# Retention and gated feed-forward on one core: columns 512 to 1023 as one block by seven quarter products, with a fourth token pair

## The chip, the cores and the metric

The kernel runs on one core of one Trainium2 chip. The metric is the device time of one execution in microseconds. Where a difference between two kernels is meant, the two are run in turn on the same chip and the ratio of their times is given.

## The reference

Inputs are q, k and v of shape (8, 8, 576, 64), that is batch, heads, tokens and head size, and three weights. All are float32; the output is (4608, 512) in float32.

```
scores = (q @ k^T) / sqrt(64)
Dmat   = gamma_h ** (i - j) where i >= j, else 0;  gamma_h = 1 - 2 ** (-5 - h)
attn   = (scores * Dmat) @ v                       # no softmax
x      = attn, heads side by side                  # (4608, 512)
out    = (sigmoid(x @ w_gate) * (x @ w_val)) @ w_out   # 512 -> 1536 -> 512
```

## The kernel before

**Columns and blocks.** x is kept transposed, 512 rows by token columns, in bfloat16. The 4608 columns are not in the order of the output rows: `rows_of` and `rows` say which output rows a column stands for. The feed-forward part goes through the columns in blocks: the first 512 columns are written out by hand, then `BLOCKS` (L366) lists two blocks of 256 columns (512 and 768) and seven of 512 (from 1024 on). TensorE's order is the order of the program: the schedule is manual, and each engine works its own list in order, waiting on semaphores.

**Retention.** Because the decay is a power, it is put into q and k by tables (`qtab`, `ktab`), and a running state per batch carries what earlier tokens give to later ones. Tokens are handled in two ways.

- A *pair* is 256 tokens of one batch, loaded with two neighbouring tokens in one partition. `PAIRS` (L102) names three: both halves of batch 0's first 512 tokens, and the first 256 tokens of batch 1. Pairs give columns 0 to 767. For a pair, `cast_pair` scales and casts (GpSimd for k and v, VectorE for q), `pair_t` turns k and q on TensorE (ScalarE copies the result out), `pair_qk` makes scores (VectorE masks them, tiles `ptp`), `third_intra` the values inside the pair, `pair_st` the state, `third_inter` the part that comes from the state, and `pair_out` and `third_out` the copies to x.
- A *step* is a chunk of 128 tokens (two pieces of 64). `STEPS` (L105) lists them; the first two are the chunks (1, 2) and (1, 3), which give columns 768 to 1023. `casts_to` loads ahead on the SP queue, scales k and q on GpSimd or VectorE, turns them (`cross`: a DMA transpose; `turn_step`, for the steps in `TURNED`, on TensorE), and casts v. `slot_of_two` does two steps at a time on TensorE: values of the two earlier ones (`intra`, `inter`), scores of the two new ones (`scores`), and what they add to the state (`products`). `after_two` adds states on VectorE and copies to x on ScalarE. Between the first and second half of `inter` a tiny operation on VectorE or ScalarE, the *glance*, reads the tile.

**Feed-forward.** A block of 256 columns is done by `h_units` (L879: per two rows of 128 of the hidden size, 8 matmuls of 256 columns for the gate, 8 for the value) and `op_units` (L1262: the output product, 512 columns a matmul). A block of 512 columns is done by `quarter_units` (L977): the product of a unit (4 x 128 hidden rows by 512 columns) is made of seven products of a quarter each, numbered 1 to 7 in the order strings. `g16` is product 6 of gate unit 1; `w03` is product 3 of value unit 0; `v9` is hidden row block 9 of the values as a plain product (`value`, L1063). Such a block needs sums of the weights (`w_sums`, tiles `wgt` and `wvt`) and four sums of x (`x_sums`, L960, tiles `xsum`): products 1, 2 and 3 read x itself, 5, 6, 7 and 4 read sums 1, 3, 2 and 4 of it in the order in which they are made. Results leave through ScalarE copies and VectorE additions (lines L999, L1044, L1052, L1055, L1040). From column 1024 on the output product of a block is also made of seven products (`quarters`, L1105), from sums of the hidden tile (`gsum`) and of the output weight (`wt_sb`).

**Order around the change.** After the first 512 columns' hidden part (`h_both`, L1325) comes their output product (`op_first`, L1484), cut into pieces between which pair 2's work stands (L1490 to L1533). Then the main loop (L1554) takes the blocks in turn. `SUMS_AT` (L1535) says at which piece of which block a weight sum, a `casts_to` or a `turn_step` is put, and `PAIRS_AT` (L1548) where the step pairs of the first four slots stand.

```
PAIRS = [(0, 0), (0, 1), (1, 0)]
STEPS = [(1, 2), (1, 3)]
BLOCKS = [(512, 256), (768, 256)] + [(t, 512) for t in range(1024, NT, 512)]
FIRST = ("g01 g05 g11 w05 g06 g15 g03 w01 g02 g16 g12 g07 w06 g13 g21 g17 w03 w11 w07 g14 g04 w02 w04 "
         "w16 w12 g26:0-1v w15:0-2v:0-3p w17 g25 g22 w13 g27:0-4v g23 w14:1-1v v8:1-2p v9:1-3v g24 v10 "
         "v11:2a1v:2a2p:2b1v:2b2p").split()
```

Of the kernel before, what the change touches and what calls it, by code (L numbers as in the profile page):

```python
# [16 lines left out]
def kernel(  # L17
# [84 lines left out]
    PAIRS = [(0, 0), (0, 1), (1, 0)]  # L102

    LAST = NC - 1
    STEPS = [(1, 2), (1, 3)]  # L105
# [59 lines left out]
    def load(s):  # L165
        b, c = STEPS[s]
        tiles = []
        for nm, src in (("k", k), ("q", q), ("v", v)):
            t = landing([P, H, D], f"{nm}32_{s}", s >= 8)
            if c < LAST:  # L170
                nc.sync.dma_start(out=t, in_=src[b, :, c * P:(c + 1) * P, :].rearrange("h p d -> p h d"))
            else:
                for j, (bj, tj) in enumerate(pieces_of(s)):
                    nc.sync.dma_start(out=t[half(j)], in_=src[bj, :, tj:tj + 64, :].rearrange("h p d -> p h d"))
            tiles.append(t)
        loaded[s] = tiles

    def load_pair(A):

        b, a2 = PAIRS[A]  # L180
        for nm, src, g in (("k", k, 0), ("q", q, 0), ("k", k, 1), ("q", q, 1), ("v", v, 0), ("v", v, 1)):
# [42 lines left out]
    LEAD_CAST = 3  # L224


    blank = lead.tile([P, P], BF16)
# [138 lines left out]
    BLOCKS = [(512, 256), (768, 256)] + [(t, 512) for t in range(1024, NT, 512)]  # L366
# [12 lines left out]
    def dealt(cols):  # L379

        return max(b for b in [(0, 0)] + BLOCKS if b[0] <= cols.start)[1] == 512

# [15 lines left out]
    def cast_pair(nm, A, g, eng):  # L398
# [3 lines left out]
        if nm != "v" and A == 2:  # L402
# [27 lines left out]
    SCALED_V = 11  # L430
    X_LATE = "ppvp"
    X_FIRST = "vvvp"
    LOOK_ACT = (0, 5, 6, 9, 10, 13, 14, 17, 18, 19, 20, 21, 22, 25, 26, 27, 29, 33, 34)
    K_ON_POOL = (13, 15, 17, 18, 19, 22, 26, 27, 28, 29)
    V_ON_ACT = ()
# [58 lines left out]
    def head(A, m, hh):  # L494

        return hh * M + m if A == 2 else 2 * m + hh

    def pair_st(A, a):
# [3 lines left out]
        for r in range(2):  # L502
            for m in range(M):
                for hh in range(2):
# [3 lines left out]
                                     stop=(a2 == 1 - b and a == 1 and r == 1 and m == M - 1),  # L508
# [42 lines left out]
    def third_intra(banks):  # L551

        for a in range(2):
            pair_tile(2, a, banks[a:a + 1])
        begun = set()
        for r in range(2):
            for u in range(2):
                for y in range(2):
                    for a in range(2):
                        for x in range(2):  # L560
                            kc = 2 * y + u
                            nc.tensor.matmul(pair_ps[4 + a][kc][0][half(x), kc, :],
                                             lhsT=natural["v", 2][half(a), r, head(2, 2 * u + x, y), :],
                                             rhs=probs["p", 2][y][half(a), 2 * u + x, r, :],
# [4 lines left out]
    def third_inter(bank):  # L569
# [9 lines left out]
        return apart  # L579

# [40 lines left out]
    TURNED = (0, 1, 7)  # L621
# [115 lines left out]
    glance = consts.tile([P, NJ], FP32)  # L737

    AGAIN = (22, 23)

    def slot_of_two(vals, news):
# [14 lines left out]
        if news:  # L756
# [7 lines left out]
            if makes:  # L764
                tiles = row_tiles(ROWS_2, f"new_{makes[0]}")
                if s < 2 * len(PAIRS_AT):
# [12 lines left out]
    def leave_two(vals, j):  # L779

        t0, n = max(b for b in BLOCKS if b[0] <= at_col[vals[0]])
        if n < 512:
            region = xT(ALL, slice(t0, t0 + n)).rearrange("p m (i j t) -> p i m j t", i=2, j=2)[:, :, :, j]
            nc.scalar.copy(out=region, in_=vals_tile[vals[0]][j].rearrange("p (i m) t -> p i m t", i=2))
            return
# [6 lines left out]
    def after_two(vals, news, i, late, first, closes):  # L792
# [16 lines left out]
        for n, s in enumerate(news):  # L809
# [3 lines left out]
            if i == n:  # L813
                add_state(s, 0)
                add_state(s, 1)
                if s < 2 * len(PAIRS_AT) and s == max(x for x in news if STEPS[x][1] < LAST):
# [31 lines left out]
    AHEAD = (2, 2, 1, 1, 0, 1, 1, 0, 1, 2, 1, 1)  # L848
# [6 lines left out]
    def casts_to(s):  # L855
        while done["cast"] <= min(NS - 1, s):
# [3 lines left out]
            cast_qk(x, 0, nc.vector if x < 2 else nc.gpsimd)  # L860
            if x not in TURNED:
                cross(x)
            cast_v(x, on_dve if x == 0 else on_act if x in V_ON_ACT else on_pool)
# [14 lines left out]

    def h_units(gvs, fcs, t0, n):  # L879

        for fc in fcs[::2]:
            gv_tile(gvs, t0, fc)
            both = made[t0, fc // 4][:, fc % 4:fc % 4 + 2, 0:n]
            for what, w_sb in (("g", wg_sb), ("v", wv_sb)):
                ps = ffn_psum.tile([P, 2, n], FP32, tag="ffn", name=f"h_{what}_{t0}_{fc}")
                for i in range(2):
                    for kc in range(NKC):
                        nc.tensor.matmul(ps[:, i], lhsT=w_sb[:, kc, (fc + i) * P:(fc + i + 1) * P],  # L888
                                         rhs=xT(kc, slice(t0, t0 + n)), start=(kc == 0), stop=(kc == NKC - 1))
                if what == "g":  # L890
                    nc.scalar.activation(out=both, in_=ps, func=AF.Sigmoid)
                else:
                    nc.vector.tensor_tensor(out=both, in0=both, in1=ps, op=ALU.mult)
                yield 8 * n
# [65 lines left out]
    def x_sums(col, engines):  # L960
# [3 lines left out]
        if len(ready[t0]) < 4:  # L964
            return
# [7 lines left out]
    def thirds(t0):  # L973

        return BLOCKS[2][0] < t0

    def quarter_units(gvs, t0):  # L977
# [85 lines left out]
        def value(fc):  # L1063
# [3 lines left out]
            for kc in range(NKC):  # L1067
                parts = 2 if t0 == BLOCKS[2][0] and kc and fc % 4 < H_CUTS else 1
# [13 lines left out]
    CASTS_AT = (13, 34)  # L1082
    SECOND = 7
    FIRST = ("g01 g05 g11 w05 g06 g15 g03 w01 g02 g16 g12 g07 w06 g13 g21 g17 w03 w11 w07 g14 g04 w02 w04 "
             "w16 w12 g26:0-1v w15:0-2v:0-3p w17 g25 g22 w13 g27:0-4v g23 w14:1-1v v8:1-2p v9:1-3v g24 v10 "
             "v11:2a1v:2a2p:2b1v:2b2p").split()
    LATER_FIRST = {0: ('2a3p', '2b3p'), 4: ('1-4v',), 9: ('2a4p', '2b4p')}
# [17 lines left out]
    def quarters(gvs, sums, t0, k):  # L1105
# [55 lines left out]
        def places(b):  # L1161
            r = b // k
# [97 lines left out]
    OP_CUTS = (6, 11, 0, 0)  # L1260
# [15 lines left out]
    def steps_of(t0):  # L1276
        return (FINAL, LATER_FINAL) if t0 + 512 == NT else (ORDER, LATER) if t0 in begun else (FIRST, LATER_FIRST)

    def ffn_units(t0, n, nxt):
        if n < 512:  # L1280
            gvs = {}
            yield from h_units(gvs, range(NFC), t0, n)
            yield from op_units(gvs, t0, n)
            return
# [6 lines left out]
        for x in order:  # L1291
# [6 lines left out]
            yield cols  # L1298
        early = None
# [179 lines left out]
    loads_to(1)  # L1479
    value_sums_begin()  # L1480
    for i in (0, 1, 3):
        w_sums("w", i, 0, nc.vector)

    def op_first(fcs, nbs, opps):  # L1484
        for fc in fcs:
            for nb in nbs:
# [7 lines left out]
    turn("q", 2, 0, *PV)  # L1494
    op_first((0, 1), (1,), opps)
    turn("k", 2, 1, *QK[0])
# [9 lines left out]
    cast_wo(10, on_act)  # L1506
    cast_wo(11, on_act)
    op_first((2, 3, 4), range(3), opps)
    pair_qk(2, 0, [TR, PV])
    pair_qk(2, 1, QK)  # L1510
    pair_st(2, 0)
# [8 lines left out]
    running[1] = new_state((1, 1, 1), FP32)  # L1520
    nc.vector.tensor_copy(out=running[1], in_=st_tiles[1])
    keep_state((1, 1, 1), running[1], on_act)
    op_first((10, 11), range(3), opps)
    store(opps[0], 0, on_dve)
    opps.append(qk_psum.tile([P, 512], FP32, tag="qk", name="op_0_3"))
    op_first(range(0, 6), (3,), opps)
    store(opps[1], P, on_act)
    op_first(range(6, 8), (3,), opps)
    turn_step(0)
    op_first(range(8, NFC), (3,), opps)  # L1530
    store(opps[2], 2 * P, on_dve)
    store(opps[3], 3 * P, on_act)
    casts_to(1)  # L1533

    SUMS_AT = ("0.0:c03p 0.0:f00p 0.3:g20p 0.3:w10v 0.3:w11v 0.6:t01p 0.7:o10p 0.8:c02v "  # L1535
# [92 lines left out]
```

## Time and profile before

| | |
|---|---|
| median of 3 runs | 306.88 us (305.95 to 307.17) |
| the profiled execution | 307.06 us, span 305.3 us |
| TensorE (PE) matmul busy | 297.9 us, 98% of the span, 4467 matmuls |
| TensorE weight loads (PEld) | 250.0 us |
| VectorE (DVE) | 224.9 us, 74% |
| ScalarE (ACT) | 204.9 us, 67% |
| GpSimd (POOL) | 226.9 us, 74% |
| DMA | 55.00 MB, mean 180 GB/s |

The span runs from the first to the last instruction of the profiled execution. A row of the timeline has the start, the length, the engine, the line, the operation with its output and inputs, and how often; in square brackets stand the idle time of the engine just before it and what ended it. The end of a matmul is modelled and includes its way through the array, so the time that a run of matmuls takes is read from the start of one group to the start of the next. SPq is the sequencer of the SP queue, which issues most DMAs.

### The profile page before, as it was taken

To read this page: it belongs to the slowest core of one execution; us is meant where nothing else is said; L and a number is where in the kernel's file an instruction comes from. 1 tells how busy PE (TensorE), PEld (TensorE's weight loads), DVE (VectorE), ACT (ScalarE), POOL (GpSimd) and SP (SyncE) were. 2 spreads that over 40 slices of the span, in tenths; PEclk is the share of its full clock that TensorE was granted. 3 is DMA by queue.
4 is the path that set the end of the run, shared out by engine and by line. 5 is a ranking of instruction groups with operands and counts; after the bars stand their busy time and mean duration, and the time that the engine had idled before them with its cause. 6 is when DMAs were issued, how large, how long until landed. Compare 5 with 4: busy or idle time off the path is not lost.

```text
span 305.3 us, 10748 instructions
## 1 busy us (share of the span) xinstructions
PE 297.9 (98%) x4467; PEld 250.0 (82%) x4467; DVE 224.9 (74%) x423; ACT 204.9 (67%) x414; POOL 226.9 (74%) x253
## 2 busy tenths in 40 slices
PE   8999999999999999999999999999999999999994
PEld 7677656878768888888888888888888888888883
DVE  6847767785886898588848974896489848935873
ACT  6855464345369657985798589857985698559830
POOL 5685554926668888999998998799969946960791
PEclk9999999999999999999999999999999999999999
DMA  7999999998999969999859966976694153004013
GB/s 207 336 330 395 371 328 225 210 153 188 203 161 222 254 127 195 228 200 248 101 132 207 256 143 151 195 206 145 147 148 158 37 187 127 2 2 137 2 37 105
DMA packets 145441, 55.00 MB, mean 180 GB/s; under 512 B 124400, under 2 KB 137712, under 8 KB 145392
## 3 DMA queue, kind: packets, MB, share of 16 engines
q1 hardware_dynamic: 144432, 53.72, 74.2%
q8 instruction: 35, 0.57, 0.8%
q10 hardware_dynamic: 960, 0.59, 0.6%
q14 instruction: 14, 0.11, 0.1%
HBM read 37.75 MB, written 9.44 MB: 155 GB/s over the span
## 4 chain that ended last, share of the span: by engine, by line
PE 80%; POOL 7%; DVE 4%; SPq 3%; DMA 2%; issue 2%; ACT 1%; POOLq 0%; DVEq 0%
PE gatea L1017 10%; PE wa L1017 10%; PE qa L1138 9%; PE qe L1138 7%; PE gatee L1017 5%; PE we L1017 5%; PE op L1269 3%; PE op L1487 3%; PE h_v L888 3%; PE hg L1337 3%; PE hv L1337 3%; PE h_g L888 3%; SPq L186 3%; PE gateg L1017 3%; PE wg L1017 2%; DMA wg<-in_moe_w_gate_dram 2%
## 5 line engine op out<-in xcount | busy, mean ns | idle before, releaser
L1040 POOL TENSOR_TENSOR gv<-gv,wu 128x512 bf16<-128x512 bf16 x20 | 24.1, 1206 | 16.4 <-DVE wu L1052 16.4
L1017 PEld LDWEIGHTS <-wg_sb 128*128 128x128 bf16 x336 | 32.9, 98 | 4.0
L1138 PEld LDWEIGHTS <-gsum 128*128 128x128 bf16 x312 | 29.9, 98 | 3.7
L1017 PEld LDWEIGHTS <-wv_sb 128*128 128x128 bf16 x296 | 28.9, 98 | 3.4
L428 POOL TENSOR_TENSOR qk<-q,qtab 128x512 bf16<-128x512 f32 x28 | 30.5, 1091 | 1.4 <-DMA q<-in_q_dram 1.4
L1052 DVE TENSOR_TENSOR gu<-gatee,gu 128x512 f32<-128x512 f32 x21 | 14.5, 691 | 23.1 <-ACT gateg L1044 10.9
L1017 PEld LDWEIGHTS <-wgt_sb 128*128 128x128 bf16 x252 | 24.6, 98 | 3.6 <-issue 0.4
L945 POOL TENSOR_TENSOR gsum<-gsum,gv 128x256 bf16<-128x256 bf16 (+1 forms) x20 | 17.9, 909 | 12.8 <-DVE gsum L945 11.1
L1017 PE MATMUL gatea<-xsum,wg_sb 128*128 128x256 bf16 x168 | 25.0, 273 | 0.0
L1138 PEld LDWEIGHTS <-gv 128*128 128x128 bf16 x228 | 21.4, 98 | 3.5 <-DVE gv L1040 0.9
L945 POOL TENSOR_TENSOR gsum<-gv,gsum 128x512 bf16<-128x512 bf16 (+1 forms) x25 | 22.9, 926 | 0.1
L428 POOL TENSOR_TENSOR qk<-k,ktab 128x512 bf16<-128x512 f32 x11 | 11.7, 1064 | 14.3 <-DMA k<-in_k_dram 10.4
L702 DVE TENSOR_TENSOR pt<-row,tri 128x512 bf16<-128x512 f32 x30 | 19.2, 682 | 3.4 <-PE row L685 3.3
L1055 DVE TENSOR_TENSOR gs<-gatea,gs 128x512 f32<-128x512 f32 x21 | 14.5, 689 | 8.5 <-PE gatea L1017 8.4
L441 POOL TENSOR_TENSOR v<-v,ktab 128x512 bf16<-128x512 f32 x19 | 20.5, 1080 | 0.0
L1017 PE MATMUL wa<-xsum,wv_sb 128*128 128x256 bf16 x136 | 20.4, 273 | 0.0
L657 ACT CAST sb<-s 128x512 bf16<-128x512 f32 (+1 forms) x26 | 14.5, 568 | 8.8 <-DVE s L831 8.7
L790 ACT CAST xT<-val 128x512 bf16<-128x512 f32 x26 | 14.7, 592 | 8.0 <-PE val L732 8.0
L945 DVE TENSOR_TENSOR gsum<-gv 128x512 bf16<-128x512 bf16 (+1 forms) x34 | 18.6, 571 | 1.5 <-POOL gv L1040 1.5
L1017 PEld LDWEIGHTS <-wvt 128*128 128x128 bf16 x168 | 16.4, 98 | 2.2 <-issue 0.2
L1040 POOL TENSOR_TENSOR gv<-gv,ws 128x512 bf16<-128x512 bf16 x14 | 16.3, 1165 | 1.6 <-DVE ws L1055 1.4
L831 DVE TENSOR_TENSOR s<-s,new 128x256 f32<-128x256 f32 x39 | 16.3, 417 | 1.6
(202 smaller groups left out, 881.9 us busy)
## 6 DMA issues: line engine op xcount, KB each, us to landing
k<-in_k_dram SPq DMA_DIRECT2D x26, 256.0 KB, 3.9
q<-in_q_dram SPq DMA_DIRECT2D x26, 256.0 KB, 4.3
v<-in_v_dram SPq DMA_DIRECT2D x26, 256.0 KB, 4.7
out_dram<-ob SPq DMA_DIRECT2D x24, 256.0 KB, 2.8
wg<-in_moe_w_gate_dram SPq DMA_DIRECT2D x12, 256.0 KB, 5.5
wv<-in_moe_w_val_dram SPq DMA_DIRECT2D x12, 256.0 KB, 5.2
wo<-in_moe_w_out_dram SPq DMA_DIRECT2D x12, 256.0 KB, 5.2
v32p<-in_v_dram SPq DMA_DIRECT2D x6, 256.0 KB, 4.6
```

Of the source, the lines that this page charges most:

```text
L428: eng.tensor_tensor(out=to, in0=by_halves(loaded[s][1 - i]), in1=tab, op=ALU.mult)
L441: nc.gpsimd.tensor_tensor(out=natural["v", s], in0=loaded[s][2], in1=tab, op=ALU.mult)
L657: eng(out=both_steps["sb", b, c][:, js], in_=both_steps["s32", b, c][:, js])
L702: nc.vector.tensor_tensor(out=t[:, y, 0:n].rearrange("p i m t -> p (i m) t"), in0=rows_tile[ss[0]][y][:, 0:n].rearrange("p i m t -> p (i m ...
L790: nc.scalar.copy(out=to, in_=src)
L831: nc.vector.tensor_tensor(out=new, in0=running[b], in1=p, op=ALU.add)
L888: nc.tensor.matmul(ps[:, i], lhsT=w_sb[:, kc, (fc + i) * P:(fc + i + 1) * P], rhs=xT(kc, slice(t0, t0 + n)), start=(kc == 0), stop=(kc == ...
L945: eng.tensor_tensor(out=to, in0=a, in1=b, op=op)
L1017: nc.tensor.matmul(ps[:, f], lhsT=w[:, kc, f * P:(f + 1) * P], rhs=x[:, kc], start=(first and f == 0 and kc == 0), stop=(f == 1 and kc == ...
L1040: eng.tensor_tensor(out=to, in0=to, in1=src, op=ALU.mult)
L1138: nc.tensor.matmul(ps[:, b], lhsT=left(fp)[:, b * P:(b + 1) * P], rhs=right(fp), start=(first and fp == 0 and b == 0), stop=(fp == NFC // ...
L1337: nc.tensor.matmul(ps[:, cols], lhsT=(wg_sb if what == "g" else wv_sb)[:, kc, fc * P:(fc + 1) * P], rhs=xT(kc, cols), start=(kc == 0), sto ...
```

## The change

Pair (1, 1), the second 256 tokens of batch 1, takes the place of the steps (1, 2) and (1, 3). Columns 512 to 1023 are then pairs 2 and 3, and are one block of 512 columns, whose gates and two of three value units are made by seven quarter products. The last four value rows (v8 to v11) and the output product (`op_units`) stay plain. In particular:

- `load_pair(3)` stands behind the last output weight on the SP queue, where the two steps' loads were. For pairs 2 and 3 the loads come in the order k, k, q, q, v, v.
- `joint_intra` is `third_intra` for either pair; `fourth_inter` adds the states to both halves of pair 3 in two rounds, with a VectorE glance between them.
- Four products of the new block (`BEGIN`: g01, g11, g02, g12), which need only pair 2's columns, stand between pair 3's steps. The other products follow in the old order (`FIRST`), with `NEXT`, the old list, for the block at 1024.
- The four sums of x for the new block are all on VectorE, directly behind pair 3's copies to x.
- Weight sums that the block needs move forward: gate unit 2's to GpSimd while the weights are still coming in, value unit 1's to VectorE between pair 2's masks.
- No step is turned on TensorE any more (`TURNED` is empty); the remaining steps have numbers two lower. Casts of v for steps 1 to 5 are placed by hand, on ScalarE and VectorE but for step 5. Three slots of steps stand in the new block's output product (`FIRST_GROUPS`).

```
-    PAIRS = [(0, 0), (0, 1), (1, 0)]
+    PAIRS = [(0, 0), (0, 1), (1, 0), (1, 1)]
-    STEPS = [(1, 2), (1, 3)]
+    STEPS = []
+    for _ in load_pair(3):
+        pass
-    BLOCKS = [(512, 256), (768, 256)] + [(t, 512) for t in range(1024, NT, 512)]
+    BLOCKS = [(t, 512) for t in range(512, NT, 512)]
...
+    def fourth_inter(other):
+        for u in range(2):
+            for a in range(2):
+                y = 1 - a if other else a
+                for x in range(2):
+                    nc.tensor.matmul(pair_ps[6 + a][2 * y + u][0][half(x), 2 * y + u, :],
+                                     lhsT=state[1, 1 + a, 1][half(y), 2 * u + x, :],
+                                     rhs=turned["qp", 3][half(y), 2 * u + x, a * P:(a + 1) * P],
+                                     start=False, stop=(u == 1), skip_group_check=True)
+        if not other:
+            looks = [pair_ps[6 + a][0][0][:, 0, 0:1] for a in range(2)]
+            nc.vector.tensor_scalar(out=glance[:, 0:1], in0=looks[0], scalar1=looks[1], scalar2=None, op0=ALU.add)
...
-    TURNED = (0, 1, 7)
+    TURNED = ()
-    AHEAD = (2, 2, 1, 1, 0, 1, 1, 0, 1, 2, 1, 1)
+    AHEAD = (3, 3, 2, 2, 1, 1)
...
+    BEGIN = "g01 g11 g02 g12".split()
+    FIRST = "g05 w05 g06 g15 g03 w01 g16 g07 w06".split() + [x.split(":")[0] for x in ON]
+    NEXT = "g01 g05 g11 w05 g06 g15 g03 w01 g02 g16 g12 g07 w06".split() + ON
...
+    for i in (0, 1):
+        w_sums("g", i, 2, nc.gpsimd)
     cast_wo(0, on_pool)
     cast_pair("k", 2, 0, nc.gpsimd)
+    w_sums("g", 3, 2, nc.gpsimd)
...
-    op_first((5, 6, 7, 8, 9), range(3), opps)
-    casts_to(0)
-    third_intra([PV, QK[0]])
-    pair_st(2, 1)
+    op_first((6, 7), range(3), opps)
+    for g in range(2):
+        cast_pair("k", 3, g, nc.gpsimd)
+    joint_intra(2, [PV, QK[0]])
     apart = third_inter(TR)
     pair_out(2, 0, on_act)
     third_out(apart)
...
+    turn("k", 3, 0, *TR)
+    turn("k", 3, 1, *PV)
+    opps.append(ffn_psum.tile([P, 512], FP32, tag="ffn", name="op_0_3"))
+    op_first(range(0, 4), (3,), opps)
+    turn("q", 3, 0, *QK[0])
+    turn("q", 3, 1, *QK[0])
+    op_first(range(4, 6), (3,), opps)
+    pair_qk(3, 0, [TR, PV])
+    op_first(range(6, 8), (3,), opps)
+    pair_st(3, 0)
+    keep_state((1, 2, 1), st_tiles[1], on_act)
+    pair_qk(3, 1, QK)
     op_first(range(8, NFC), (3,), opps)
     store(opps[3], 3 * P, on_act)
...
+    ahead()
+    joint_intra(3, FF)
+    fourth_inter(False)
+    ahead()
+    fourth_inter(True)
+    pair_out(3, 0, on_act)
+    pair_out(3, 1, on_dve)
+    x_sums(FROM - P, "vvvv", 1)
+    ahead()
+    pair_st(3, 1)
+    keep_state((1, LAST - 1, 1), st_tiles[1], on_act)
+    ahead()
...
+    FIRST_GROUPS = {0: ([], [0, 1]), 4: ([0, 1], [2, 3]), 8: ([2, 3], []), 11: ([], [4, 5])}
```

More of the change, by code (lines that the diff above doesn't have):

```diff
@@ L379, in dealt @@
     def dealt(cols):
[L381 removed]
+        return cols.start >= FROM
     def x_out(rows_, cols):
@@ L1081 @@
     EARLY = ((11, "g01"), (13, "g05"))
-    CASTS_AT = (13, 34)
+    CASTS_AT = (4, 20, 34)
     SECOND = 7
[L1084 to L1087, printed above, removed]
+    ON = ("g13 g21 g17 w03 w11 w07 g14 g04 w02 w04 "
+          "w16 w12 g26:0-1v w15:0-2v:0-3p w17 g25 g22 w13 g27:0-4v g23 w14:1-1v v8:1-2p v9:1-3v g24 v10 "
+          "v11:2a1v:2a2p:2b1v:2b2p").split()
+    BEGIN = "g01 g11 g02 g12".split()
+    FIRST = "g05 w05 g06 g15 g03 w01 g16 g07 w06".split() + [x.split(":")[0] for x in ON]
+    NEXT = "g01 g05 g11 w05 g06 g15 g03 w01 g02 g16 g12 g07 w06".split() + ON
+    LATER_FIRST = {}
+    LATER_NEXT = {0: ('2a3p', '2b3p'), 4: ('1-4v',), 9: ('2a4p', '2b4p')}
     ORDER = ("g02 g06 g11 w05 g03 w01 g15 g07 g16 g12 w06 g13 w02 g21 g17 w11 w03 w07v g22 g04 g26 w04 "
@@ new lines, with ahead @@
+    gvs = {}
+    begun[t1] = gvs, *quarter_units(gvs, t1)
+    early = iter(BEGIN)
+    def ahead(n=1):
+        for _ in range(n):
+            x = next(early)
+            begun[t1][1](x[0], int(x[1]), int(x[2]))
+    ahead()
[10 more added lines that the diff above has]
+    ahead()
```

171 lines of the change are left out of this document (82 added, 89 removed), and 3 rows, old and new, of the table SUMS_AT.

## The prediction

> **What bounds the kernel now.** I read the page's totals and slices first, then the waits of TensorE, then the timeline of TensorE through the stretch that the change rewrites.
>
> ```profile
> span 305.3 us, 10748 instructions
> PE 297.9 (98%) x4467; PEld 250.0 (82%) x4467; DVE 224.9 (74%) x423; ACT 204.9 (67%) x414; POOL 226.9 (74%) x253
> ...
> PEclk9999999999999999999999999999999999999999
> ```
>
> TensorE is busy for 98% of the span, at full clock in all 40 slices. DVE, ACT and POOL have a quarter or more of theirs free. So the time is the TensorE work plus the few places where TensorE waits. In the rewritten stretch (33 to 126 us) the list of waits names just three such places. In the timeline they are:
>
> ```profile
> 55.69 1.03 PE L888 MATMUL h_g<-xT,wg_sb 128*128 128x256 bf16 x8 [0.37 <-DVE gv L893]
> ...
> 81.59 0.31 PE L732 MATMUL val<-T,sb 64*64 64x64 bf16 x12 [0.16 <-DVE glance L755]
> ...
> 90.44 0.60 PE L1017 MATMUL gatee<-xsum,wgt_sb 128*128 128x256 bf16 x4 [0.20 <-DVE xsum L971]
> ```
>
> A change here is worth the matmuls that it removes plus these 0.37 + 0.16 + 0.20 = 0.73 us, less every new wait that it makes. Behind column 1024 the seven-product blocks keep their order of products and show no TensorE wait, so nothing is to be won or lost there.
>
> **TensorE work of the feed-forward part.** The two 256-column blocks are 96 gate and 96 value matmuls of 256 columns:
>
> ```profile
> 59.63 1.04 PE L888 MATMUL h_g<-xT,wg_sb 128*128 128x256 bf16 x8
> 60.50 1.04 PE L888 MATMUL h_v<-xT,wv_sb 128*128 128x256 bf16 x8
> ```
>
> Eight start 0.87 us apart from the next eight, 0.109 us each. The new block has gates in three units of 7 quarter products of 4 matmuls (84). Values take two such units (56), and the last four value rows stay plain: v8 to v11 are 16 matmuls of 512 columns, worth 32. That is 172 for 192: 20 x 0.109 = 2.18 us less. The output product of these columns stays plain (48 of 512 columns in both kernels), so it gives nothing.
>
> **TensorE work of attention.** Two single chunks and three turns on TensorE go; a pair comes. The nearest rows, each pair of starts giving the length of the work between them:
>
> ```profile
> 66.60 0.32 PE L716 MATMUL val<-pt,v 64*64 64x64 bf16 x16
> ...
> 67.91 2.79 PE L1269 MATMUL op<-wo_sb,gv 128*128 128x512 bf16 x23
> ```
> ```profile
> 50.35 0.61 PE L629 MATMUL turn<-ident,qk 128*128 128x128 bf16 x8
> 50.80 1.03 PE L1487 MATMUL op<-wo_sb,gv 128*128 128x512 bf16 x4
> ```
> ```profile
> 38.21 0.39 PE L465 MATMUL kTp<-ident,kp 128*128 128x128 bf16 x4
> 38.44 0.38 PE L1487 MATMUL op<-wo_sb,gv 128*128 128x512 bf16 x1
> ...
> 42.22 0.64 PE L484 MATMUL qkp<-qT,kT 64*64 64x128 bf16 x32
> 42.69 0.42 PE L505 MATMUL st<-vp,kp 64*64 64x64 bf16 x16
> 43.04 3.41 PE L1487 MATMUL op<-wo_sb,gv 128*128 128x512 bf16 x15
> 46.38 0.64 PE L562 MATMUL pvp<-ptp,vp 64*64 64x128 bf16 x32
> 46.86 0.32 PE L505 MATMUL st<-vp,kp 64*64 64x64 bf16 x10
> ```
>
> Removed: the 128 small matmuls of two chunks, 67.91 - 66.60 = 1.31 us, and three turns of 0.45, together 2.66 us. Added: four transposes of 0.23 (0.92), 32 score products (0.47), 32 state products (2 x 0.35), 32 value products (0.48), and 16 products with the states at the value products' 0.015 (0.24): 2.81 us. Attention costs 0.15 us more; with slower state products it is 0.5. TensorE's work falls by 2.18 - 0.15 = 2.03 us.
>
> **Loads and GpSimd.** Pair 3 is loaded at the place of the SP queue where the two chunks were, first issue at 39.20:
>
> ```profile
> 39.20 0.38 SPq L171 DMA_DIRECT2D k<-in_k_dram  x1
> ...
> 46.03 0.86 SPq L171 DMA_DIRECT2D v<-in_v_dram  x1
> ```
> ```profile
> 29.23 0.61 POOL L308 CAST wv_sb<-wv 128x512 bf16<-128x512 f32 x1 [0.68 <-DMA wv<-in_moe_w_val_dram]
> ...
> 44.92 1.04 POOL L428 TENSOR_TENSOR qk<-k,ktab 128x512 bf16<-128x512 f32 x1 [1.67 <-ACT sb L650]
> ...
> 50.25 0.61 POOL L443 CAST v<-v 128x512 bf16<-128x512 f32 x1 [1.33 <-DMA v<-in_v_dram]
> ...
> 58.28 1.15 POOL L364 TENSOR_TENSOR wgt_sb<-wg_sb 128x512 bf16<-128x512 bf16 x1
> ```
>
> Even at the chunks' pace (sixth load there at 50.25, about 1.1 us apart) the sorted order k, k, q, q, v, v gives converted k near 47 and converted v near 51. Laid end to end, TensorE wants them at 48.3 and 51.4. GpSimd also gets three gate sums (1.15 us each, the row at 58.28) among the conversions from 31 us on, where it idles for up to 0.7 us ahead of each cast for want of loads. Both are hidden, narrowly, so I cost them at nothing; if the covers fell short by half a microsecond each, that would be 1 us, inside the range. The remaining chunk loads move about 5 us later, and their first scores from 62.34 in the old order to about 74, so the turns by DMA instead of TensorE (the median transpose lands in 4.2 us by the list of DMA issues) are hidden too. Their conversions, though, now fall beside pair 3, which matters below.
>
> ```profile
> T<-qk SPq DMA_TRANSPOSE x27, 4.2
> 62.34 0.45 PE L685 MATMUL row<-T 64*64 64x64 bf16 x32
> ```
>
> **New waits in the pair-3 chain.** This is where the gain can leak. Pair 3 is a serial chain TensorE, ACT, TensorE, DVE, TensorE, ACT and DVE, DVE, TensorE, with only pieces of the first block's output product and four early gate products (g01, g11, g02, g12, which need pair 2's columns alone) as cover.
>
> ```profile
> 42.68 2.48 DVE L491 TENSOR_TENSOR ptp<-qkp,trip 128x512 bf16<-128x512 f32 x4 [1.82 <-PE qkp L484]
> ```
> ```profile
> L475 ACT COPY qT<-qTp 128x512 bf16<-128x512 bf16 x6 | 4.4, 738 | 0.1
> L790 ACT CAST xT<-val 128x512 bf16<-128x512 f32 x26 | 14.7, 592 | 8.0 <-PE val L732 8.0
> ```
>
> Pair 2's value products now come 9 output matmuls and 16 state products (about 2.3 us) behind the last scores, and the four masks take 2.48 us from the first scores: wait about 0.1. Pair 3's scores wait for the qT copy, which stands behind an output copy and two kT copies on ACT: 0.1. Pair 3's value products stand 1.3 us behind the last scores, of whose group two masks remain to be made: 0.25. The glance between the two halves of the products with the states costs 0.05, covered by g11. Together 0.5 us, estimated from these rows; if every cover suffices it is 0, and with doubled handoffs 1.0.
>
> Then the block's four sums of x on DVE. They need both of pair 3's columns: ACT's copy of the first is queued behind its copy for g11. By the durations the first sum can start near 55.9, and TensorE, after g12, wants it at the same time. With d the time of one sum, the wait for the first sum (g05) is d + 0.1 and the wait for the third (g06, behind g05 and w05, 0.87 us) is 2d - 0.87, if positive. The trace has the same sums in the same role, before the 1024 block, and elsewhere:
>
> ```profile
> 89.97 0.75 DVE L971 TENSOR_TENSOR xsum<-xT 128x512 bf16<-128x512 bf16 x2
> 90.64 0.42 DVE L971 TENSOR_TENSOR xsum<-xT,xsum 128x512 bf16<-128x512 bf16 x1
> ```
> ```profile
> L971 DVE TENSOR_TENSOR xsum<-xT,xsum x7: 419/1127/1360, 90.6 to 272.5; 128x512 bf16<-128x512 bf16 x7
> ```
> ```profile
> 56.15 0.52 DVE L364 TENSOR_TENSOR wvt<-wv_sb 128x512 bf16<-128x512 bf16 x1
> 56.70 1.15 DVE L364 TENSOR_TENSOR wvt<-wvt,wv_sb 128x512 bf16<-128x512 bf16 x1
> ```
> ```profile
> 56.34 1.22 POOL L428 TENSOR_TENSOR qk<-q,qtab 128x512 bf16<-128x512 f32 x1
> ...
> 91.80 0.61 POOL L443 CAST v<-v 128x512 bf16<-128x512 f32 x1 [1.70 <-DMA v<-in_v_dram]
> ```
>
> So d is 0.42 where GpSimd pauses (it stood idle for 1.70 us up to 91.80) and 1.15 where GpSimd is at a conversion. The waits are 0.5 us at d = 0.42, 1.7 at 0.83 and 3.4 at 1.39. I take 0.5, the row of the same sums in the same role, and keep 3.4 as the other end.
>
> [...]
>
> **The sum.** The profiled execution took 307.06 us (span 305.3); the median is 306.88, 0.18 below. Work -2.03, old waits -0.73, chain +0.5, sums +0.5: -1.76, so 305.3 for an execution like the profiled one and 305.1 against the median. A measurement of this kernel can tell about 0.5% (1.5 us) from no change.
>
> **Rivals.** *The gain is spent on the sums, half colliding.* With d at 0.83, the mean of 0.52 and 1.15, the sums cost 1.7 us and the net is -0.5: 306.4. For it: the chunk conversions moved to just this time. Against it: they are paced by loads 1.1 us apart, and GpSimd has no v conversions for chunks 1 to 4, so it should pause.
>
> *DVE against GpSimd makes it slower.* If GpSimd always has its next operation ready, each sum waits for one. At d = 1.39 the sums cost 3.4 us; DVE ends its fourth sum and the weight sum behind it 3.4 us later than in the old row against g05, and has about 2.6 us of idle time in the next stage (1.74, 0.53 and 0.36 before its next three gate sums), so 0.5 to 0.8 more comes through late bank releases; with the chain at 1.0 the net is 2.0 to 2.5: about 309.1. Break-even lies near d = 0.94. For it: the median 1127 ns. Against it: the row at 90 us.
>
> ```profile
> 93.47 0.69 DVE L1052 TENSOR_TENSOR gu<-gatee,gu 128x512 f32<-128x512 f32 x1 [1.74 <-ACT gu L999]
> 95.44 0.69 DVE L1055 TENSOR_TENSOR gs<-gatea,gs 128x512 f32<-128x512 f32 x1 [0.53 <-PE gatea L1017]
> 96.50 0.69 DVE L1052 TENSOR_TENSOR gu<-gatee,gu 128x512 f32<-128x512 f32 x1 [0.36 <-PE gatee L1017]
> ```
>
> That the change does less than it says is in the sum already: a quarter of the value rows and the whole output product stay plain.
>
> **How the numbers follow.** The forecast (d near 0.42, 305.1) gets 0.46, the half-colliding case 0.36, the slower case 0.18. The forecast's own range is 303.9 (no new waits except 0.3 at the sums, and work 0.3 better) to 305.9. The range of all reaches 307.6, which is d = 1.1 with the chain at 0.9. Faster by over 0.5% is 0.46, within 0.5% 0.36, slower 0.18.
>
> **What would show it.** TensorE busy down by about 2 us, to 296; the first gate product of column 1024 near 87.9 us instead of 89.65, and the pitch of the later blocks as before. In the list of waits: gatee of the new block behind xsum, 0.5 us in the forecast, 1.5 or more in the rivals, with xsum rows of 0.42 or about 1.1. The prediction is wrong if TensorE waits for pair 3's loads or conversions, if the later blocks get waits that they did not have, or if the new block's products wait for banks.

## The result, and the profile after

The changed kernel took 318.55 us (median of three, 317.84 to 320.13) against 306.88 (305.95 to 307.17): 1.040 times the time before, 95% interval 1.033 to 1.047. The prediction was 305.1 us, with a range of 303.9 to 307.6. It is 13.5 us out, and on the other side of no change. One execution of a later run (the scores earlier, 318.09 us) was a slow one, and the time of that run is given without it.

The profiled execution of the changed kernel is one of 318.55 us. Its page begins:

```profile
span 316.8 us, 10647 instructions
...
PE 297.9 (94%) x4392; PEld 245.5 (77%) x4402; DVE 230.4 (73%) x421; ACT 213.6 (67%) x431; POOL 238.7 (75%) x261
```

TensorE is busy as long as before (297.9 us), with 65 matmuls fewer in the program (by the weight loads, 4402 for 4467, all of which are recorded; the records of ten matmuls are missing here), and idle for 18.9 us where it was idle for 7.4. The table of stretches says where: each begins at the same product in both kernels (the first product of column block 0's output; the first gate product of columns 1024, 1536, 2048 and 2560). The columns are the stretch, its length, and the busy time of TensorE, its weight loads, VectorE, ScalarE and GpSimd with the number of their instructions, then granted clock, DMA share and GB/s. Before:

```profile
38.00:89.65 51.65, 51.12 (x875) 37.50 (x874) 38.92 (x71) 24.19 (x46) 32.32 (x36) 1.00 1.02 217
89.65:119.75 30.10, 29.90 (x473) 25.70 (x472) 24.92 (x48) 22.66 (x46) 23.92 (x26) 1.00 0.92 195
119.75:150.38 30.63, 30.55 (x503) 26.92 (x500) 24.64 (x44) 23.44 (x48) 29.33 (x30) 1.00 1.02 186
150.38:180.85 30.47, 30.47 (x503) 26.94 (x501) 23.56 (x44) 23.70 (x49) 27.88 (x31) 1.00 0.82 190
```

After:

```profile
39.25:94.29 55.04, 50.04 (x803) 32.92 (x808) 43.62 (x70) 33.35 (x65) 41.18 (x43) 1.00 1.02 227
94.29:126.50 32.21, 30.32 (x479) 25.77 (x473) 25.93 (x48) 22.53 (x46) 23.55 (x25) 1.00 0.81 184
126.50:158.86 32.36, 30.53 (x502) 27.02 (x500) 24.78 (x44) 23.14 (x47) 29.96 (x31) 1.00 0.78 165
158.86:190.87 32.01, 30.70 (x502) 26.91 (x500) 22.85 (x44) 23.85 (x49) 27.42 (x30) 1.00 0.75 169
```

The loss is 1.25 us ahead of the first row, 3.39 in the rewritten stretch (-1.76 was forecast), 2.11 in the block of column 1024, 1.73 and 1.54 in the next two, 1.51 in the three after these (91.04 us became 92.55), nothing in the last: 11.5 us. More than half lies in stretches whose products the change does not touch. The waits of TensorE over 0.5 us behind the first output product, from the timeline:

```profile
60.21 0.61 PE L1014 MATMUL gatee<-xsum,wgt_sb 128*128 128x256 bf16 x4 [0.93 <-DVE xsum L968]
62.57 0.60 PE L1014 MATMUL gatea<-xsum,wgt_sb 128*128 128x256 bf16 x4 [1.31 <-DVE xsum L968]
66.68 0.60 PE L1014 MATMUL wa<-xsum,wvt 128*128 128x256 bf16 x4 [1.33 <-ACT wg L1041]
97.68 0.60 PE L1014 MATMUL gatea<-xsum,wgt_sb 128*128 128x256 bf16 x4 [1.01 <-ACT gateg L1041]
150.88 0.27 PE L1139 MATMUL qe<-wo_sb,gv 128*128 128x256 bf16 x1 [1.83 <-issue]
184.24 0.49 PE L1139 MATMUL qa<-wt_sb,gsum 128*128 128x256 bf16 x3 [1.20 <-POOL gsum L942]
219.20 0.26 PE L711 MATMUL new<-v,qk 64*64 64x64 bf16 x8 [0.56 <-issue]
250.72 0.28 PE L750 MATMUL val<-T,sb 64*64 64x64 bf16 x8 [0.77 <-issue]
```

Three groups can be told apart: the x sums and the copy behind them (3.57 us), one copy in the block of column 1024 (1.01), and four waits in later blocks (4.36), three of which wait for nothing that the profile knows. "Issue" is the word for that. The rows of the sums, with GpSimd beside them:

```profile
58.79 2.55 DVE L968 TENSOR_TENSOR xsum<-xT 128x512 bf16<-128x512 bf16 x2 [0.19 <-ACT xT L637]
61.26 2.44 DVE L968 TENSOR_TENSOR xsum<-xT,xsum 128x512 bf16<-128x512 bf16 x2
```
```profile
59.83 1.22 POOL L432 TENSOR_TENSOR qk<-k,ktab 128x512 bf16<-128x512 f32 x1
61.02 1.22 POOL L432 TENSOR_TENSOR qk<-q,qtab 128x512 bf16<-128x512 f32 x1
62.20 1.22 POOL L432 TENSOR_TENSOR qk<-k,ktab 128x512 bf16<-128x512 f32 x1
```

Each x2 row is two sums, so a sum takes about 1.25 us here, in step with GpSimd's conversions, which run without a pause.

### The profile page after: what moved, and what is told of

Its sections match the earlier page's. It is cut to its first block, busy times and chain, and to the rows that moved or that the text cites. A ratio compares the mean times of both kernels' runs of the same rounds, so it can differ in the third digit from the quotient of the medians.

```text
span 316.8 us, 10647 instructions
## 1 busy us (share of the span) xinstructions
PE 297.9 (94%) x4392; PEld 245.5 (77%) x4402; DVE 230.4 (73%) x421; ACT 213.6 (67%) x431; POOL 238.7 (75%) x261
## 4 chain that ended last, share of the span: by engine, by line
PE 72%; DVE 10%; ACT 4%; issue 4%; POOL 4%; SPq 3%; DMA 2%; ACTq 0%; DVEq 0%; POOLq 0%
PE gatea L1014 11%; PE qa L1139 10%; PE wa L1014 9%; PE qe L1139 8%; PE gatee L1014 5%; PE we L1014 5%; SPq L187 3%; PE gateg L1014 3%; PE hg L1340 3%; PE hv L1340 3%; PE op L1272 3%; PE wg L1014 2%; POOL gsum L942 2%; DVE xsum L968 2%; DMA wg<-in_moe_w_gate_dram 2%
## 5 line engine op out<-in xcount | busy, mean ns | idle before, releaser
L1014 PEld LDWEIGHTS <-wg_sb 128*128 128x128 bf16 x384 | 37.2, 98 | 4.9 <-issue 0.2
L1014 PEld LDWEIGHTS <-wv_sb 128*128 128x128 bf16 x328 | 32.1, 98 | 3.7
L1014 PEld LDWEIGHTS <-wgt_sb 128*128 128x128 bf16 x288 | 28.0, 98 | 7.8 <-issue 3.0
L1014 PE MATMUL gatea<-xsum,wg_sb 128*128 128x256 bf16 x192 | 28.5, 273 | 0.0
L1014 PE MATMUL wa<-xsum,wv_sb 128*128 128x256 bf16 x152 | 22.8, 273 | 0.0
L1014 PEld LDWEIGHTS <-wvt 128*128 128x128 bf16 x192 | 18.8, 98 | 4.3 <-issue 2.1
L1035 ACT ACTIVATE gv<-gu 128x512 bf16<-128x512 f32 x24 | 15.3, 639 | 7.7 <-DVE gu L1049 7.7
L968 POOL TENSOR_TENSOR xsum<-xT 128x512 bf16<-128x512 bf16 x12 | 13.6, 1156 | 7.1 <-ACT xT L803 5.0
L1037 POOL TENSOR_TENSOR gv<-gv,ws 128x512 bf16<-128x512 bf16 x16 | 18.8, 1176 | 0.3 <-DVE ws L1052 0.3
L1035 ACT ACTIVATE gv<-gs 128x512 bf16<-128x512 f32 x24 | 15.2, 632 | 5.3 <-DVE gs L1052 5.3
```

Of the source, the lines that this page charges most:

```text
L968: (nc.gpsimd if by == "p" else nc.vector).tensor_tensor(out=to, in0=a, in1=b, op=ALU.subtract)
L1014: nc.tensor.matmul(ps[:, f], lhsT=w[:, kc, f * P:(f + 1) * P], rhs=x[:, kc], start=(first and f == 0 and kc == 0), stop=(f == 1 and kc == ...
L1035: nc.scalar.activation(out=to, in_=src, func=AF.Sigmoid)
L1037: eng.tensor_tensor(out=to, in0=to, in1=src, op=ALU.mult)
```

## The experiments

The ratios are to the kernel before, run on the same chip beside it.

| run | median us (lowest to highest) | ratio, 95% interval |
|---|---|---|
| changed kernel, again | 319.73 (319.03 to 320.78) | 1.044 (1.040 to 1.047) |
| changed, later instructions shifted | 313.16 (311.23 to 313.86) | 1.019 (1.013 to 1.025) |
| before, later instructions shifted | 312.22 (311.35 to 312.87) | 1.017 (1.012 to 1.022) |
| changed, last sum on GpSimd | 316.08 (314.91 to 318.63) | 1.031 (1.024 to 1.037) |
| changed, scores earlier | 314.45 (312.62 to 316.50) | 1.025 (1.017 to 1.033) |
| three repairs together | 310.38 (309.46 to 310.76) | 1.012 (1.009 to 1.016) |
| and w06 later | 309.08 (308.22 to 310.16) | 1.009 (1.006 to 1.012) |
| and room for the copies | 309.12 (307.77 to 310.79) | 1.008 (1.005 to 1.012) |

**The same kernel again.** The base line, and the 1.25 us of the lead-in.

> The changed kernel itself again, beside the two, as their base line: 318.5 by the first result (317.5 to 319.5). In the first profile TensorE waited 0.88 us more in the lead-in, ahead of any changed instruction, for GpSimd's conversion of a load that landed late. Theory (a late load of that one execution): here the first output product starts near 37.8 us as in the kernel before, not at 39.0, while the waits at the instruction blocks (near 150, 184, 219 and 250 us) and at the sums are all there again. Rival (the changed order of loads or of code delays the lead-in): it starts near 39 again.

319.73 us; the first output product starts at 37.58 us. So the 1.25 us were of one execution; a late load, which is what the profile named, fits, and the order of the change does not make it. The time is no shorter for it, since something else came in: TensorE's granted clock fell to half for 3.4 us twice, from 60.70 us (0.4 us behind the longer wait for the sums) and from 149.45 (0.2 us behind the first wait at a block). Four products took 0.85 us there in place of 0.44, so each time cost up to 1.7 us. The first profile has no such stretch at the same waits; why the clock fell is not shown. Over the span it was 0.987, and 0.987 to 0.999 in the executions of the changed kernel, where the kernel before had 0.997 to 1.0.

The later waits are all there again. The columns of this view are as above, for stretches from the start to the end of each later wait; the first count is that of the matmuls:

```profile
0.00:149.25 149.25, 141.01 (x2014) 106.97 (x2015) 114.84 (x212) 96.78 (x189) 115.12 (x136) 0.99 0.94 236
0.00:184.44 184.44, 174.63 (x2526) 135.83 (x2527) 139.22 (x259) 121.80 (x241) 144.19 (x166) 0.98 0.89 220
0.00:188.44 188.44, 178.46 (x2654) 139.09 (x2655) 140.09 (x261) 124.29 (x245) 147.63 (x169) 0.98 0.88 217
0.00:220.49 220.49, 209.13 (x3166) 166.12 (x3167) 163.04 (x302) 148.40 (x296) 173.87 (x196) 0.98 0.86 209
0.00:251.77 251.77, 239.90 (x3678) 193.22 (x3679) 186.12 (x344) 171.90 (x344) 199.91 (x224) 0.99 0.83 201
```

2014, 2526, 2654, 3166, 3678: the steps are 512, 128, 512 and 512. At these five places TensorE stops a multiple of 256 instructions apart (128 matmuls and 128 weight loads are 256), whatever comes there: a product with gv, one with gsum, a state product. In the 2.4 us up to the end of the wait at 184.45 the DMA queues moved, as the view of DMA by queue has it (packets, MB, share of the engines' time):

```profile
q1 hardware_dynamic: 361, 0.09, 17.5%
q8 instruction: 1, 0.02, 2.5%
```

One packet of 16 KB, 64 bytes for each of 256 instructions. The records of this queue have it landed at 183.20 us; TensorE went on 1.25 us later. Counted from these places, 128 weight loads a block, the block in front of it was begun at 180.29 and its last weight load came 2.43 us later, since all but 12 of its products are 64-row ones, 8 to 17 ns apart. The four long waits (2.28, 1.46, 1.38 and 0.52 us) stand behind blocks run through in 1.30, 2.43, 1.12 and 2.94 us, and the next block could be used 2.7 to 4.2 us after the last one was begun (1.9 to 3.9 in the first profile). In the kernel before no block takes less than 3.65 us (3.35 if the count begins three loads earlier, as in the expectation of its own shifted run), and there is no such wait.

**The changed kernel with its later instructions shifted.**

```
-    OP_CUTS = (0, 0, 0, 0)
+    OP_CUTS = (0, 11, 11, 11)
+    OP_QUARTERS = (0, 0, 0, 11)
...
-                parts = 2 if 0 < fc <= OP_CUTS[(t0 - BLOCKS[0][0]) // P + nb] else 1
+                parts = 4 if 0 < fc <= OP_QUARTERS[nb] else 2 if 0 < fc <= OP_CUTS[nb] else 1
```

> The changed kernel with 33 of the 512-column matmuls of columns 512 to 1023's output product cut into narrower ones (22 into halves, 11 into quarters): 55 more weight loads and 55 more matmuls for the same columns, so TensorE's work is the same to 0.1 us, but every later instruction stands 110 places further on in TensorE's stream. Theory A (instruction blocks): TensorE's instructions come in transfers of 16 KB (256 instructions), each asked for when the block before it is begun, and a block that is run through in less than about 3.5 us makes TensorE wait for the next. The changed kernel has five such blocks (1.1 to 3.3 us), with waits of 1.83, 1.20, 0.56 and 0.77 us at exactly 256-instruction steps; with the shift no block is shorter than 3.7 us. A expects these four waits gone, 4.4 us less: about 314.2 us (313.5 to 315.5). Theory B (the waits belong to the work around them: the sums on GpSimd, DMA landings): nothing but 55 instructions changed, so 318.5 (317.5 to 320), and the waits at 150.9 and 184.2 us still there.

313.16 us, 5.4 less than the first result and 6.6 less than the repeat. This is 0.3 us below the forecast range. In the profile the way from column 1024's first gate product to the end is 218.2 us, where the first profile had 222.5: 4.3 less, for 4.4 forecast. All that is left in TensorE's list of waits above 0.5 us is the blank tile at the start, the sums, three waits for qT copies (0.8 together) and the 1.0 us of the block of column 1024:

```profile
PE gatea L1014 <- DVE xsum L968: 1.3, 1, 1.3
PE idle L245 <- DVE blank L232: 1.1, 1, 1.1
PE gatea L1014 <- ACT gateg L1041: 1.0, 1, 1.0
PE qkp L488 <- ACT qT L479: 0.8, 3, 0.4
PE gatee L1014 <- DVE xsum L968: 0.6, 1, 0.6
```

The wait that the profile had put down to GpSimd's gsum (1.20 and 1.46 us) is gone too, though nothing on GpSimd changed. In the first profile the last gsum ended at 183.54 us, 0.70 us before TensorE went on. The 1.33 us for ACT's copy of wg are not in the list either; TensorE's clock was at half for 3.4 us just ahead of that product, from 60.50 us, which would have let ACT catch up.

**The kernel before, shifted the wrong way.**

```
-    OP_CUTS = (6, 11, 0, 0)
+    OP_CUTS = (6, 11, 11, 11)
+    OP_QUARTERS = (0, 0, 0, 11)
...
-                parts = 2 if 0 < fc <= OP_CUTS[(t0 - BLOCKS[0][0]) // P + nb] else 1
+                piece = (t0 - BLOCKS[0][0]) // P + nb
+                parts = 4 if 0 < fc <= OP_QUARTERS[piece] else 2 if 0 < fc <= OP_CUTS[piece] else 1
```

> The kernel before with 33 output matmuls of columns 768 to 1023 cut into narrower ones (the third tile's in halves, the fourth's in quarters): 44 more matmuls and weight loads, the same columns, TensorE's work the same to 0.1 us, nothing else changed. Theory A (instruction blocks): the kernel before has no block that is run through in less than 3.35 us; with this shift six of the later ones take 1.6 to 3.5 us by the order of its instructions, so waits that the profile can put down to nothing appear in the attention stretches of the later blocks, 3 to 6 us together: about 311.5 us (310 to 313). Theory B: 306.9 (306 to 307.5), no new waits.

312.22 us, 5.7 over the kernel before. In the profile the way from column 1024's first gate product to the end grew from 215.6 to 221.2 us, by 5.5, and waits appear where there were none:

```profile
144.79 0.39 PE L1138 MATMUL qa<-wt_sb,gsum 128*128 128x256 bf16 x2 [0.65 <-issue]
...
148.52 0.26 PE L732 MATMUL val<-T,sb 64*64 64x64 bf16 x8 [0.65 <-issue]
...
181.12 0.50 PE L1138 MATMUL qa<-wo_sb,gsum 128*128 128x256 bf16 x3 [1.34 <-issue]
...
213.80 0.39 PE L1138 MATMUL qa<-wo_sb,gsum 128*128 128x256 bf16 x2 [2.32 <-issue]
```
```profile
0.00:144.70 144.70, 140.50 (x2137) 113.48 (x2143) 112.28 (x215) 89.17 (x176) 104.32 (x128) 1.00 0.97 242
0.00:148.50 148.50, 143.58 (x2265) 116.08 (x2271) 114.81 (x221) 91.64 (x180) 108.12 (x132) 1.00 0.96 237
0.00:181.10 181.10, 174.84 (x2777) 143.44 (x2783) 139.00 (x266) 116.22 (x231) 136.79 (x162) 1.00 0.93 224
0.00:213.79 213.79, 205.19 (x3289) 170.13 (x3295) 160.57 (x306) 141.03 (x282) 163.55 (x189) 1.00 0.91 216
```

The weight loads, all of which are recorded, stand at 2143, 2271, 2783 and 3295. Each leaves 95 when divided by 128, and so do 2015, 2527, 2655, 3167 and 3679 in the changed kernel: the same places in the stream of two different programs. Nearly the same edit takes 5 us from one kernel and gives as much to the other, so it is not the extra instructions that cost, but where the 256-instruction steps fall. That settles what the waits are.

How long a block takes does not settle by itself whether TensorE waits. Of the six short blocks that the expectation counted here, four made waits of 0.65 to 2.32 us; the other two, run through in 2.20 and 2.40 us, made none above 0.2 us. The packet of the next block had landed 0.2 and 0.9 us after these two were begun, and 2.5 to 2.7 us after the four. What makes it land early or late was not tested.

Theory A has each block asked for when the one before it is begun. In the profiles of the kernel before (35 packets) and the changed kernel (34) a packet began to move 1.0 us (median) behind the nearest counted beginning of a block, from 2.2 us ahead of it to 2.9 behind; the request itself has no record. Behind no block above 3.7 us was there such a wait here; behind blocks of 1.1 to 3.1 us the wait was mostly 0.5 to 2.3 us.

**The last sum of x on GpSimd.**

```
-    x_sums(FROM - P, "vvvv", 1)
+    x_sums(FROM - P, "vvvp", 1)
```

> The changed kernel with the last of the four sums of x for columns 512 to 1023 on GpSimd in place of DVE. GpSimd then stands in front of this sum, idle, until DVE has made the other three, and its conversions of the chunks after the first come behind it. Theory C (DVE's sums are slowed by GpSimd's work on SBUF beside them): the three sums on DVE take about 0.42 us each in place of 1.27, the waits for the sums (0.93 and 1.31 us) go to at most 0.3 and 0.1, the wait of 1.33 us for ACT's copy shrinks with them to at most 0.5: 2.5 to 3.3 us less, about 315.6. Rival D (a DVE sum of this size takes 1.2 us here by itself, because it reads tiles that ACT and DVE have just written): the sums stay above 1 us and the time within 0.8 us of 318.5.

316.08 us: 2.5 less than the first result, 3.7 less than the repeat. DVE's rows and GpSimd's:

```profile
56.91 0.76 DVE L968 TENSOR_TENSOR xsum<-xT 128x512 bf16<-128x512 bf16 x2 [0.19 <-ACT xT L637]
57.59 0.42 DVE L968 TENSOR_TENSOR xsum<-xT,xsum 128x512 bf16<-128x512 bf16 x1
```
```profile
58.15 1.20 POOL L968 TENSOR_TENSOR xsum<-xT,xsum 128x512 bf16<-128x512 bf16 x1 [4.12 <-ACT gv L1035]
```

With GpSimd idle (4.12 us ahead of its own sum) the same operations take 0.38 to 0.42 us in place of 1.25, and both waits for the sums are gone. That is theory C. The wait for ACT's copy shrank from 1.33 to 0.69 us, not to 0.5, and 0.45 and 0.29 us came up behind it: in this block DVE and ACT are close to TensorE's pace even without the collision.

**The scores of chunks 4 and 5 earlier.**

```
-    FIRST_GROUPS = {0: ([], [0, 1]), 4: ([0, 1], [2, 3]), 8: ([2, 3], []), 11: ([], [4, 5])}
+    FIRST_GROUPS = {0: ([], [0, 1]), 4: ([0, 1], [2, 3]), 8: ([2, 3], [4, 5])}
```

> The changed kernel with the scores and state products of the third pair of chunks (4 and 5) issued with the values of the second (three quarters through the output product of columns 512 to 1023) in place of directly ahead of column 1024's first gate product. Theory E (the wait of 1.01 us for ACT's copy in the block of column 1024 comes from that place: DVE's two masks, then the state sum, then ACT's state copy, in front of the gate copy): the wait at 97.7 us goes and so does most of the 0.22 us behind it: 1.0 to 1.5 us less, about 317.3. Rival: the wait is a part of the general lateness (ACT and DVE behind since the sums of columns 512 to 1023), and stays within 0.4 us.

314.45 us, 4.1 under the first result with a spread of 3.9 us, and lower than the 317.3 expected. The time alone cannot be split, since the waits at the instruction blocks moved by up to 1.6 us between executions (0.56, 1.38 and 2.12 us at the same place in three profiles). The stretch itself can. In the changed kernel the chain of DVE and ACT runs up to the copy:

```profile
94.29 1.29 DVE L720 TENSOR_TENSOR pt<-row,tri 128x512 bf16<-128x512 f32 x2
95.50 0.41 DVE L846 COPY s<-new 128x256 f32<-128x256 f32 x1
96.02 0.42 DVE L844 TENSOR_TENSOR s<-s,new 128x256 f32<-128x256 f32 x1
```
```profile
96.53 0.62 ACT L675 CAST sb<-s 128x512 bf16<-128x512 f32 x1 [2.06 <-DVE s L844]
97.05 0.58 ACT L1041 COPY gateg<-gatea 128x512 f32<-128x512 f32 x1
```

With the scores earlier the state copy has been made before the first gate product, and the product that waited 1.01 us starts without such a wait. (In the run with the sum on GpSimd, where the sums held nobody, it was still 1.01 us, so it does not come from them.)

```profile
93.82 0.27 PE L1014 MATMUL gatea<-xsum,wgt_sb 128*128 128x256 bf16 x1
```

The 0.22 us for ACT's wg behind it stayed, against what was expected.

**The three repairs together,** with the cuts chosen anew (`OP_CUTS = (11, 8, 4, 0)`, `OP_QUARTERS = (0, 0, 0, 11)`).

> The changed kernel with the edits of the three runs that each took a part of the loss back, together: the last sum of x on GpSimd, chunks 4 and 5 scored with the second pair of chunks, and 56 output matmuls' worth of cuts chosen anew for this order (11, 8 and 4 matmuls of the first three tiles in halves, 11 of the fourth in quarters), so that no later block of 256 instructions takes less than 3.4 us. If the three losses are separate: 5 us from the blocks, 2.5 from the sums and 1.2 from the scores come off about 318, so 309.3 (308.3 to 310.5), still 2 to 3 us over the kernel before, whose waits in the rewritten stretch were smaller. If they overlap (the sums' delay had hidden the wait for the copy, or the blocks' waits only move): 311 to 313.

310.38 us, near the upper end of the first case. One wait at a block was left in the profile, behind a block that the expectation had at 3.4 us or more and whose weight loads took 2.94:

```profile
89.43 0.34 PE L1273 MATMUL op<-wo_sb,gv 128*128 128x128 bf16 x3 [1.03 <-issue]
```

**w06 later, and then room for the copies.**

```
-    FIRST = "g05 w05 g06 g15 g03 w01 g16 g07 w06".split() + [x.split(":")[0] for x in ON]
+    FIRST = "g05 w05 g06 g15 g03 w01 g16 g07 g13 g21 w06".split() + [x.split(":")[0] for x in ON[2:]]
...
-    SUMS_AT = ("0.0:w02v 0.1:c01p 0.2:g22p 0.4:c02p 0.6:v01a 0.9:w12v 0.10:c03p 0.11:v02v "
+    SUMS_AT = ("0.0:w02v 0.0:w12v 0.1:c01p 0.2:g22p 0.4:c02p 0.6:v01a 0.10:c03p 0.11:v02v "
```

> The previous kernel with the product w06 of columns 512 to 1023 put two products later (behind g13 and g21) and the weight sum for w12 made on DVE directly behind the first weight sum in place of between two gate sums. In the run with the sum on GpSimd TensorE waited 0.69 us for ACT's copy ahead of w06, 0.45 us for DVE's gate sum ahead of g14 (DVE had been held 1.26 us by that weight sum beside a GpSimd conversion), and 0.29 us for DVE's ws. If these waits have the causes named, 1.0 to 1.4 us come off: about 308.1, at the border of what can be told from the kernel before. If ACT and DVE are simply full in this block, the waits move to the next products and the time stays within 0.4 us of the previous kernel's.

309.08 us: 1.3 less, as much as was forecast, from a higher start; but in the profile 1.0 of this is the block wait above, which did not recur, in this run or the next, though the block again took 2.94 us. The three waits (0.69, 0.44 and 0.29 us in the run before) became one:

```profile
64.89 0.60 PE L1014 MATMUL wa<-xsum,wv_sb 128*128 128x256 bf16 x4 [1.09 <-ACT wu L996]
```

The last run puts w06 behind g13 alone and moves one value conversion from ACT to DVE (`0.6:v01a` becomes `0.14:v01v`).

> The previous kernel (three repairs, w12's weight sum early) with w06 one product earlier (behind g13 alone) and the conversion of the second chunk's values on DVE, later, in place of ACT. In the previous kernel ACT had no idle time from 58 to 65 us, and TensorE waited 1.09 us for its copy wu ahead of w07. If ACT's queue is what holds TensorE here, 0.61 us of conversion less and the copy one product earlier take 0.6 to 0.9 us off: 308.3 (307.8 to 308.7), with at most 0.4 us of waits left in columns 512 to 1023; still above the kernel before, since the pair's chain costs about 1 us more there and columns 1024 to 1535 about 0.4, against 2.6 us less work. If the wait only goes to another copy: 309.1, and ACT's place in this block is full.

309.12 us: no gain in the median. In its profile the waits of this block are 0.25, 0.15 and 0.27 us and the way from the first output product to the end is 0.6 us shorter, but two waits in the lead-in for GpSimd's conversions of loaded tiles (0.78 and 0.99 us; 0.14 and 0.25 in the run before) took it back. Whether the 0.6 us are there cannot be told. No version beat the kernel before; the best is 0.8 to 0.9% slower.

## Why the prediction was wrong, step by step

**Later blocks unchanged.** This is the step that failed most. The prediction said that behind column 1024 nothing is to be won or lost because the order of products stays and TensorE shows no wait there. Nearly all of the order stayed; the place of each product in the instruction stream did not, as the program has 65 matmuls and weight loads fewer by then, 17 of them because it no longer cuts 17 output products in two (`OP_CUTS` was (6, 11, 0, 0)). Cost 4.4 us in the first profile, 5.8 in the second (2.28, 1.46, 0.17, 1.38 and 0.52); shown by the shifts in both kernels. No rival held it. The kernel before had no wait there with every block at 3.65 us and more; shifted, it had waits too.

**The sums of x.** Mis-sized, with the mechanism of the slower rival. Forecast: d = 0.42 and 0.5 us, because GpSimd, paced by loads, should pause. GpSimd did not pause, d was 1.25, and the waits were 0.93 and 1.31 us, with 1.33 more for ACT's copy of wg: 3.6 us. By its formula the prediction gave 1.35 and 1.63 for the two sums at this d; TensorE was itself later than assumed. The rival had 3.4 for the sums and 0.5 to 0.8 for lateness behind them. No run shows its d of 1.39; the longest of these sums in the changed kernel's profile took 1.37 us. The median that spoke for the rival (1.13) was near the 1.25 measured, and the row that the forecast preferred (0.42 at a pause of GpSimd) was true only of that pause. The break-even was wrong too: by the prediction's own terms it lies near d = 1.01, not 0.94, still below the 1.25 measured.

**Column 1024.** "As before" was wrong: 1.01, 0.22 and 0.46 us of waits. The first comes from the place of the last scores, shown by moving them. The other two were not tested.

**The chain of pair 3.** About right in size. The waits at its places are 0.22 us for the qT copy (0.1 forecast), none at the values of either pair (0.35 forecast) and none at the glance; 0.16 us of "issue" stand twice where a train of small products gives way to a wide one. Loads and conversions of pair 3 held nobody: this step was right.

**TensorE's work.** Forecast: 2.0 us less. In the rewritten stretch TensorE was busy 50.04 us for 51.12, 1.1 less, and 296 us in all was wrong by 1.9. Busy time is a poor gauge here, though: a product of 0.109 us pitch that nothing follows counts 0.27 us, so each new wait adds some 0.16 us of busy time.

The repeat, whose trace has all matmuls, can be taken apart from start to start; its rewritten stretch is 3.0 us longer than before. The products of 256 and 512 columns, each at its own pitch (0.109 and 0.216 us), come to 39.4 us for 41.7: 2.2 less, as forecast, so this step was right. The transposes and small products took 9.2 us for 8.8, with their waits. The gaps at the wide products are 4.8 us longer: 2.1 are the two waits for sums (there is none for ACT's copy; TensorE was at half clock ahead of it), 1.7 the half clock, less 0.4 of the old wait, and the other 1.4 are gaps of 0.3 us and less, which the prediction had at nothing. What makes these small gaps was not tested.

**The lead-in.** 1.25 us that belong to one execution.

The repaired kernel shows the same from the other side. With w06 later it is still 2.3 us over the kernel before. In its profile the rewritten stretch is 0.5 us longer than before, with 2.1 us less of wide products: small products and transposes take 0.7 us more, the gaps at wide products 1.8, of which 1.09 are the wait for wu. So the gain of the seven products is spent inside the stretch, and the blocks from column 1024 on take another 1.1 us, of which 0.22 and 0.48 are the two waits whose causes were not tested.

## What to carry to other kernels

When a change moves the number of TensorE's instructions, lay out what each 256 of them (matmul and weight load both count) take, through the whole program; a train of 128 small products that falls between two steps can make TensorE wait where nothing was edited (mostly 0.5 to 2.3 us here), and cutting a few wide products into narrower ones shifts the steps at no cost in work that TensorE's busy time shows (297.5 us with 44 matmuls more in the kernel before, six of the 4511 not recorded, where it was 297.9). A DVE sum of SBUF tiles is to be priced by what GpSimd has queued beside it at that moment (0.42 or 1.25 us here), not by its best row. Ask of each "issue" wait whether its distance from the next is a multiple of 128 matmuls, before looking for a cause among the engines.

## What the runs showed of the hardware that was not expected

- TensorE's instructions arrive in blocks of 256, 16 KB each, on a queue of their own (34 packets for the changed kernel's 4402 matmuls and 4402 weight loads); the next was usable 1.9 to 4.2 us after the one before was begun, and most blocks run through in 1.1 to 3.1 us cost 0.5 to 2.3 us (four of 2.2 to 2.9 us cost 0.2 us or nothing). In the waits TensorE went on 1.2 to 1.6 us after the packet had landed. Moving the steps was worth 5 to 6 us of 310, in either direction.
- Such a wait can carry the name of another engine (GpSimd's gsum, 1.20 and 1.46 us), and its length changes from execution to execution by more than a microsecond.
- TensorE's granted clock was half for 3.4 us soon after some waits of 1.3 us and more (twice in the repeat, once with the later instructions shifted), and four products took 0.85 us there in place of 0.44; the same waits in the first profile had no such stretch.
- A bf16 sum of 128x512 on DVE took 0.38 to 0.42 us with GpSimd idle and 1.25 us beside its conversions.
